# A planned first batch in which a load from DRAM waits, in the plan, for the landing of the store in front of it

## The chip, the cores and the metric

The kernel runs on one core of one Trainium2 chip. The metric is the device time of one execution in microseconds; three runs of the kernel before took 928.23, 928.39 and 931.25 us, median 928.39 us.

## The reference

A sparse attention of the Longformer kind feeds a two-layer feed-forward network, all in float32. There are 8 batches, 8 heads, 512 local and 32 global positions, and 64 elements in a head.

```python
s_g = scale * q_g @ k_all.T;  out_g = softmax(s_g) @ v_all      # 32 global rows see everything
mask = abs(pos[:, None] - pos[None, :]) <= 32                   # local rows: a band and the globals
s_l = concat([scale * q_l @ k_g.T, where(mask, scale * q_l @ k_l.T, -1e9)])
out_l = softmax(s_l) @ concat([v_g, v_l])
x = concat([out_g, out_l])                                      # 4608 tokens x 512
h = x @ w_in                                                    # 512 x 2048
g = maximum(h, 0) + alpha * minimum(h, 0)
out = g @ w_out                                                 # 2048 x 512
```

## The kernel before, in words

**Tiling.** The tokens form nine groups, one for the local tokens of each batch (512 tokens) and one for all global tokens. A group runs through 16 feed-forward blocks f of 128 hidden units. Step f1 makes the hidden block (h_ps) from the tokens, step f2 adds its part to the four output banks (o). f2 has two parts: fa uses the upper half gh of the activation (8 matmuls), fb the lower half gl (4 matmuls). Every float32 factor is split into an upper and a lower part, so that three products stand for one. Attention works on pairs P of heads, four to a batch and 32 in all. A batch's pairs must be through before its group's f1 steps begin.

**Weights.** The weights come as raw float64 words (`wraw`, 32 loads Lw of 512 KB) and are decoded on the chip in the first group's time: cv and ab on ScalarE (ACT), d1, d2, d3 on VectorE (DVE), ia on GpSimd (POOL), ca on ACT, su on DVE. Decoded second-layer weights are stored to DRAM (`wo`, and `wa` beside it), sums of first-layer weights too (`wf`), and read again in later groups.

**One pair in the first batch's time.** S makes the scores (s_ps). Pairs 0 to 3 are transposed on TensorE (T, Tg). Pairs 4 to 7 belong to batch 1 and go another way: red masks the scores into the tile `p` on DVE, ex exponentiates on ACT, nm normalises on POOL, and tq transposes 32x32 blocks in place on DVE. Then sq stores `p` to DRAM in four DMAs (tile `scratch`), and hq loads it back in the transposed layout (tile `pt`). The global part goes the same way: tr, sr (four DMAs from `sg_sb`) and hr. V multiplies `pt` with the values into o_ps, and G makes the next pair's global scores. The red step of pair P+1 overwrites `p` and so waits for sq of pair P. On the chip hq waits for the landing of sq's stores, and hr for that of sr's.

**What sets the order.** Nearly all DMAs of this stage, loads, stores and fetches, are issued by SyncE (SP) in program order. The order of the first batch's steps on each engine is written by a list scheduler, the class `Plan` (L59): `early` (L153) declares each step with engine, cost, needed steps, buffers taken and freed, and sometimes a due time. `due_times` (L70) works a due time back to every step and subtracts a bias by the step's name. `run` (L95) walks a model of the five engines: at each turn it takes the engine whose next step can start first, and on it, among the steps that could start within `near` of that time, the one with the earliest due time. Its start time is the end of each needed step plus a lag (L112). For two entries of SP that lag is -100: they count as ready at once. A DMA is taken to start 1.6 us after issue or behind the one before it, to last its `cost`, and to be seen 0.8 us later (L130, L131). The order that comes out is pinned; on the chip each engine follows it and waits where a step isn't ready. `issue` (L893) turns a name into instructions, `scatter` (L618) and `fetch_pt` (L629) are sq/sr and hq/hr. From block 16 on (L1114) the order is written in other functions, `slow_unit` and `fast_unit`, and left to the framework's own scheduler where not pinned. The numbers of the plan stand in LIST (L38): `first`, `pace`, `pair0` and `pair` set due times, `bias` shifts them.

Of the kernel before, what the change touches and what calls it, by code (L numbers as in the profile page):

```python
# [35 lines left out]
GOFF = 1024  # L36
GROWS = {1: (0, 0), 4: (0, 1), 7: (0, 2), 10: (1, 0), 13: (1, 1), 15: (1, 2)}
LIST = dict(  # L38
    first=37.579, pace=5.504, pair0=70.66, pair=20.171, slack=2, vsub=1, ahead=4, inflight=4, near=0.1, vgl=1, half=True,
    bias=dict(tq=-6, V=12, ex=-3, ca=-3, hr=6, gz=0, xB=12, hq=-1, Lw=-7, sr=12, ab=3, gsc=0, Lq=-6, be=5, rzr=1, yh=3, gexp=-12, cv=-1, ia=1, xA=3, red=-3),  # L40
)
FAST = range(2 * NF, NB * NF)
CATCH = (16, 23, 30)
# [15 lines left out]
class Plan:  # L59
# [3 lines left out]
        self.slots = {k: [0.0] * n for k, n in slots.items()}  # L63
        self.ops, self.slack, self.near, self.bias = {}, slack, near, bias

    def op(self, name, engine, cost, needs=(), lock=False, take=(), free=(), kind=None, due=None, n=1):
        assert name not in self.ops, name
        self.ops[name] = dict(engine=engine, cost=cost, needs=[x for x in needs if x], lock=lock, take=take, free=free, kind=kind, due=due, n=n)

    def due_times(self):  # L70
        users = {n: [] for n in self.ops}
# [23 lines left out]
    def run(self):  # L95
        ops, users = self.ops, self.due_times()
        end, order = {}, []
        free = dict(PE=5.4, ACT=2.5, DVE=5.0, POOL=4.0, SP=1.2)
        lock, dma, kind = 0.0, 3.3, None
        left = {n: len(o["needs"]) for n, o in ops.items()}  # L100
        ready = {n for n, k in left.items() if k == 0}
        while ready:
            can = []
            for n in sorted(ready):
                o = ops[n]
                e = o["engine"]
                if any(len(self.slots[p]) < k for p, k in o["take"]):
                    continue
                t = free[e]
                for x in o["needs"]:  # L110
                    y = ops[x]["engine"]
                    lag = (0.12 if e != "SP" else -100.0) if y == e else 0.3 if y == "PE" else 0.12  # L112
                    t = max(t, end[x] + lag)
                for p, k in o["take"]:
                    t = max(t, sorted(self.slots[p])[k - 1])
                if o["lock"]:
                    t = max(t, lock)
                can.append((t, o["at"], n))
            assert can, sorted(ready)
            t, _, n = min(can)  # L120
            e = ops[n]["engine"]
            t, _, n = min((c for c in can if ops[c[2]]["engine"] == e and c[0] <= t + self.near), key=lambda c: (c[1], c[0]))
            o = ops[n]
            cost = o["cost"]
            if e == "PE":
                cost = cost * (1.25 if t < 45 else 1.0) + (0.3 if kind != o["kind"] else 0.0)
                kind = o["kind"]
            if e == "SP":
                free[e] = t + 0.48 * o["n"]
                dma = max(dma, t + 1.6) + cost  # L130
                stop = dma + 0.8  # L131
            else:
                free[e] = stop = t + cost
                if o["lock"]:
                    lock = stop
            for p, k in o["take"]:
                for _ in range(k):
                    self.slots[p].remove(min(self.slots[p]))
            for p, k in o["free"]:
                self.slots[p] += [stop] * k  # L140
            end[n] = stop
            order.append(n)
            ready.discard(n)
            for u in users[n]:
                left[u] -= 1
                if left[u] == 0:
                    ready.add(u)
        assert len(order) == len(ops)
        self.end, self.order = end, order
        return order  # L150


def early(first, pace, pair0, pair, slack, vsub, ahead, inflight, near, vgl=0, half=False, bias={}):  # L153

    plan = Plan({"st": NST - 2, "w": NWB}, slack, near, bias)
    op = plan.op
    for P in range(9):
        pre = P < NRAW
        op(f"Lq{P}", "SP", 1.72, [f"G{P-2}", f"S{P-2}"] if P > 1 else [])
        if pre and P % 2:  # L160
            op(f"Lv{P}", "SP", 2.62, [f"S{P-1}"], take=(("w", 2),))
        else:
            op(f"Lv{P}", "SP", 2.62, [f"V{P-1 if P > NRAW else P-2}"] if P else [])
        due = pair0 + pair * (P - 5) if P > 4 else None
# [32 lines left out]
        last = first + pace * 15.5 if P == 8 else None  # L197
        if not pre:
            op(f"tq{P}", "DVE", 1.23, [f"nm{P}.0", f"nm{P}.1"], due=last)
            op(f"sq{P}", "SP", 1.31, [f"tq{P}"], n=4, due=last)  # L200
        if P == 8:
            break
        pb = [f"V{P-1}"] if P else []
        if pre:
            op(f"T{P}", "PE", 1.1, [f"nm{P}.0", f"nm{P}.1"] + ([f"pt0{P-1}", f"pt1{P-1}"] if P else []), kind="t", free=(("w", 1),) if P % 2 else ())
            op(f"pt0{P}", "ACT", 0.49, [f"T{P}"] + pb)
            op(f"pt1{P}", "DVE", 0.60, [f"T{P}"] + pb)
            op(f"Tg{P}", "PE", 0.45, [f"gsc{P}", f"T{P}", f"ptg{P-1}" if P else None], kind="t")
            op(f"ptg{P}", "ACT", 0.40, [f"Tg{P}"] + pb)
            lb = [f"pt0{P}", f"pt1{P}", f"ptg{P}"] + ([f"ex{P+1}.0", f"ex{P+1}.1"] if P < 3 else ["xlA1", "xlB1", "xg1"])  # L210
        else:
            op(f"tr{P}", "DVE", 0.5, [f"gsc{P}", "clear"])
            op(f"hq{P}", "SP", 1.31, [f"sq{P}"] + pb)
            op(f"sr{P}", "SP", 0.5, [f"tr{P}"], n=4)
            op(f"hr{P}", "SP", 0.5, [f"sr{P}", f"hq{P}"])
            lb = [f"hq{P}", f"hr{P}", f"mem{P+1}", f"Lq{P+1}"]
        op(f"V{P}", "PE", 2.0, [f"Lv{P}"] + lb, kind="v", free=(("w", 2),) if pre and P % 2 else ())
        if not pre:
# [7 lines left out]
        if not pre:  # L226
            c = P - NPAIR
# [8 lines left out]
    for k in range(2 * NF):  # L236
        f, j = divmod(k, 2)
# [12 lines left out]
    for t in range(NF):  # L250
        x = [f"xl{a}{P}" for P in range(NPAIR) for a in "AB"]
# [37 lines left out]
def longformer_ffn(ctx: ExitStack, tc: tile.TileContext, qk, v, w, alpha, out):  # L289
    nc = tc.nc  # L290
    pin, pin_sync = [True], [True]
    vec, act, pool = (Engine(tc, e, pin) for e in (nc.vector, nc.scalar, nc.gpsimd))
# [28 lines left out]
    sync = Engine(tc, nc.sync, pin_sync)  # L321
# [267 lines left out]
    def new_pt(P):  # L589
        if P not in pts:  # L590
            pts[P] = work.tile([128, 1408], F32, tag="pt", name="pt", bufs=1)
        return pts[P]
# [17 lines left out]
    scratch = {}  # L610

    def transpose_dve(P, x):
        t, n = (ps[P], 1024) if x == 0 else (sg_sb, 384)
        for e in range(0, n, 512):
            seg = t[:, e : min(n, e + 512)]
            vec.transpose(seg, seg)

    def scatter(P, x):  # L618
        t, n = (ps[P], 1024) if x == 0 else (sg_sb, 384)
        scratch[P, x] = dram.tile([4, 32, 4, n // 4], F32, tag=f"scratch{x}", name="scratch", bufs=2)  # L620
        for c in range(4):
            src = t[32 * c : 32 * c + 32, :].rearrange("k (j n) -> k j n", j=4)
            sync.dma_start(scratch[P, x][:, :, c, :].rearrange("j k n -> k j n"), src)

    def transpose_q(P, x):
        transpose_dve(P, x)
        scatter(P, x)

    def fetch_pt(P, x):  # L629
        sc = scratch.pop((P, x)).rearrange("j k c n -> (j k) (c n)")  # L630
        o, n = ((0, 1024), (GOFF, 384))[x]
        sync.dma_start(new_pt(P)[:, o : o + n], sc)

    def pv_all(P, first, last):
        vv, t = vs.pop(P), pts.pop(P)
# [247 lines left out]
    def begin():  # L883
# [3 lines left out]
        def parts(name):  # L887
            for k in ("tq", "sq", "hq", "tr", "sr", "hr", "Lq", "Lv", "Lw", "red", "mn", "ex", "rza", "rzr", "nm", "mem", "gm", "gexp", "gz", "gsc", "pt0", "pt1", "ptg", "Tg", "xlA", "xlB", "xA", "xB", "xg", "yh", "yl", "cv", "ab", "d1", "d2", "d3", "ia", "ca", "su", "wf", "wo", "f1", "fa", "fb", "gh", "gl", "S", "T", "V", "G", "p", "n", "mk", "al", "be"):
                if name.startswith(k) and name[len(k) :].replace(".", "").isdigit():
                    return k, name[len(k) :]  # L890
            return name, ""

        def issue(name):  # L893
            k, rest = parts(name)
            if k in ("red", "mn", "ex", "rza", "rzr", "nm"):
                P, h = map(int, rest.split("."))
# [7 lines left out]
            n = int(rest)  # L904
# [6 lines left out]
            if k in ("mk", "al", "be"):  # L911
                return
            if k in ("tq", "tr", "sq", "sr", "hq", "hr"):
                {"t": transpose_dve, "s": scatter, "h": fetch_pt}[k[0]](n, "qr".index(k[1]))
                return
            if k in ("cv", "ab", "d1", "d2", "d3", "ia", "ca", "su"):
                key = divmod(n, 2)
# [42 lines left out]
            elif k in ("xlA", "xlB"):  # L960
                a, src = (slice(0, 384), outs[n][0][:, 0:384]) if k == "xlA" else (slice(384, 512), outs[n][1][:, 0:128])
# [28 lines left out]
            else:  # L990
                raise KeyError(name)

        plan = early(**LIST)
        for name in plan.run():
            issue(name)
# [118 lines left out]
    for t in range(NF, NT + LAG):  # L1114
        G, f = divmod(t, NF)
# [75 lines left out]
```

## Time and profile before

| what | value |
|---|---|
| median of three runs | 928.39 us |
| the profiled execution's own time | 927.88 us |
| its span, first to last instruction | 926.1 us |
| TensorE busy | 885.9 us (96%) |
| VectorE busy | 608.7 us (66%) |
| ScalarE busy | 388.6 us (42%) |
| GpSimd busy | 312.7 us (34%) |
| mean granted TensorE clock | 0.972 |
| moved by DMA | 211.19 MB, mean 228 GB/s |

How to read it: PE is TensorE (PEld its weight loads), DVE is VectorE, ACT is ScalarE, POOL is GpSimd and SPq the DMA-issuing queue of SyncE. In a row of a timeline stand the start, the duration, engine, line, operation, what it writes and reads, how many were merged, and in brackets the idle time before it with what ended it. A row of waits names who waited for whom, the total, how often and the longest. Nearly all engine instructions have L280 and all matmuls L309, two helpers, so rows are told apart by their tiles. The work of the plan ends at about 180 us of the span.

### The profile page before, as it was taken

To read this page: it belongs to the slowest core of one execution; us is meant where nothing else is said; L and a number is where in the kernel's file an instruction comes from. 1 tells how busy PE (TensorE), PEld (TensorE's weight loads), DVE (VectorE), ACT (ScalarE), POOL (GpSimd) and SP (SyncE) were. 2 spreads that over 40 slices of the span, in tenths; PEclk is the share of its full clock that TensorE was granted. 3 is DMA by queue.
4 is the path that set the end of the run, shared out by engine and by line. 5 is a ranking of instruction groups with operands and counts; after the bars stand their busy time and mean duration, and the time that the engine had idled before them with its cause. 6 is when DMAs were issued, how large, how long until landed. Compare 5 with 4: busy or idle time off the path is not lost.

```text
span 926.1 us, 22539 instructions
## 1 busy us (share of the span) xinstructions
PE 885.9 (96%) x8668; PEld 764.9 (83%) x8668; DVE 608.7 (66%) x1676; ACT 388.6 (42%) x1166; POOL 312.7 (34%) x275
## 2 busy tenths in 40 slices
PE   7798968999999999999999999999999999999998
PEld 5676646787888888888888888888888899899898
DVE  5887757877577666866677667766686656544532
ACT  6877655553444433443345333443344322211211
POOL 3444433255444333433223323322343322222221
PEclk7889889799999999999999999999999999999999
DMA  8968977999665866586667667586657552645630
GB/s 306 348 178 322 341 252 271 337 362 358 232 208 177 294 210 197 189 277 217 211 228 253 230 224 225 187 262 217 201 181 269 185 192 91 205 160 180 205 116 24
DMA packets 86811, 211.19 MB, mean 228 GB/s; under 512 B 23985, under 2 KB 44465, under 8 KB 82865
## 3 DMA queue, kind: packets, MB, share of 16 engines
q1 hardware_dynamic: 86704, 209.76, 67.0%
q8 instruction: 68, 1.11, 0.5%
q14 instruction: 39, 0.31, 0.1%
HBM read 165.95 MB, written 43.78 MB: 226 GB/s over the span
## 4 chain that ended last, share of the span: by engine, by line
PE 67%; DMA 13%; DVE 9%; ACT 6%; SPq 2%; issue 2%; POOL 0%; DVEq 0%; ACTq 0%
PE o L309 30%; PE h_ps L309 28%; PE o_ps L309 4%; ACT p L280 3%; DMA scratch<-sg_sb 3%; PE s_ps L309 3%; DMA wraw<-in_w_dram 2%; PE g_ps L309 2%; DVE g L280 2%; DMA scratch<-p 2%; SPq L280 2%; DVE xl L280 2%; DMA pt<-scratch 1%; DMA alpha_sb<-in_alpha_dram 1%; DVE x_raw L280 1%
## 5 line engine op out<-in xcount | busy, mean ns | idle before, releaser
L280 POOL TENSOR_TENSOR gl<-g,gh 128x512 fp32r<-128x512 f32 (+1 forms) x128 | 159.1, 1243 | 375.8 <-ACT gh L280 306.0
L309 PE MATMUL h_ps<-xh,wt 128*128 128x256 f32 (+1 forms) x1120 | 241.0, 309 | 4.1 <-DVE wt L280 3.7
L309 PE MATMUL o<-gh,wo 128*128 128x512 f32 (+1 forms) x1024 | 244.3, 381 | 0.0
L280 ACT CAST gh<-g 128x512 fp32r<-128x512 f32 (+1 forms) x144 | 85.8, 596 | 306.5 <-DVE g L280 304.2
L309 PEld LDWEIGHTS o<-gh,wo 128*128 128x128 f32 x1024 | 176.8, 188 | 31.9 <-issue 0.4
L309 PEld LDWEIGHTS h_ps<-xh,wt 128*128 128x128 f32 x1120 | 182.4, 189 | 24.4 <-issue 6.1
L309 PE MATMUL h_ps<-xl,wt 128*128 128x256 f32 (+1 forms) x560 | 171.6, 306 | 0.8 <-DVE xl L280 0.8
L309 PE MATMUL o<-gl,wo 128*128 128x512 f32 (+1 forms) x512 | 131.1, 378 | 0.0
L280 DVE TENSOR_SCALAR g<-h_ps,alpha_sb 128x512 f32<-128x512 f32 (+1 forms) x128 | 91.5, 715 | 41.1 <-PE h_ps L309 35.4
L309 PEld LDWEIGHTS h_ps<-xl,wt 128*128 128x128 f32 x560 | 105.8, 189 | 6.6 <-DVE xl L280 1.0
L309 PE MATMUL h_ps<-xh,s 128*128 128x256 f32 x576 | 105.4, 279 | 2.9 <-DVE h_ps L280 2.0
L309 PEld LDWEIGHTS o<-gl,wo 128*128 128x128 f32 x512 | 92.8, 188 | 18.4
L280 POOL TENSOR_TENSOR p<-p,rz 128x512 f32<-128x512 f32 x64 | 69.2, 1101 | 101.1 <-DVE rz L280 95.2
L309 PEld LDWEIGHTS h_ps<-xh,s 128*128 128x128 f32 x576 | 90.7, 188 | 8.1 <-issue 4.0
L280 DVE TENSOR_TENSOR h_ps<-u,h_ps 128x256 f32<-128x256 f32 x144 | 61.1, 424 | 49.1 <-PE h_ps L309 47.5
L280 ACT ACTIVATE p<-p,mn 128x128 f32<-128x128 f32 x224 | 86.9, 396 | 4.8 <-DVE mn L280 4.8
L280 DVE SCALAR_TENSOR_TENSOR g<-h_ps,g 128x512 f32<-128x512 f32 (+1 forms) x128 | 84.1, 657 | 4.2
L309 PE MATMUL h_ps<-xl,s 128*128 128x256 f32 x288 | 80.6, 280 | 0.9 <-DVE xl L280 0.7
L280 DVE TENSOR_TENSOR u<-u,h_ps 128x256 f32<-128x256 f32 x96 | 40.3, 420 | 62.1 <-PE h_ps L309 38.7
L280 POOL TENSOR_TENSOR wt<-wt,wr 128x512 int32<-128x512 int32 x32 | 45.8, 1433 | 93.4 <-DVE wt L280 73.4
L309 PE MATMUL o_ps<-pt,v 128*64 128x32 f32 (+1 forms) x1600 | 59.8, 234 | 15.2 <-DMA pt<-scratch 13.2
L309 PEld LDWEIGHTS o_ps<-pt,v 128*64 128x64 f32 x1600 | 55.2, 149 | 22.4 <-DMA pt<-scratch 10.7
(88 smaller groups left out, 1046.1 us busy)
## 6 DMA issues: line engine op xcount, KB each, us to landing
wo<-wo SPq DMA_DIRECT2D x128, 512.0 KB, 4.4
v<-in_v_dram SPq DMA_DIRECT2D x30, 1024.0 KB, 5.8
qk<-in_qk_dram SPq DMA_DIRECT2D x32, 672.0 KB, 7.0
wraw<-in_w_dram SPq DMA_DIRECT2D x32, 512.0 KB, 7.4
scratch<-p SPq DMA_DIRECT2D x112, 128.0 KB, 3.0
pt<-scratch SPq DMA_DIRECT2D x28, 512.0 KB, 5.5
wo<-wt SPq DMA_DIRECT2D x16, 512.0 KB, 8.5
out_dram<-ost SPq DMA_DIRECT2D x32, 256.0 KB, 3.3
```

What stands on the lines that cost most here:

```text
L280: ins = op(*a, **k)
L309: ins = nc.tensor.matmul(*a, **k)
```

## The change

The lag between two SP entries stays at -100 except for steps whose name begins with h, which are hq and hr: they now start 0.12 us after the modelled end of the steps that they need, sq and for hr also sr and hq. The same line makes the lag between two TensorE steps 0.3 instead of 0.12. TensorE costs after 45 us are multiplied by 1.05, a DMA starts 2.0 instead of 1.6 us after issue. A step can now be a DMA issued by ACT (`dma=`), for names in `aq`; LIST sets `aq=""`, so all of them stay on SP. The numbers in LIST are others.

```diff
 LIST = dict(
-    first=37.579, pace=5.504, pair0=70.66, pair=20.171, slack=2, vsub=1, ahead=4, inflight=4, near=0.1, vgl=1, half=True,
-    bias=dict(tq=-6, V=12, ex=-3, ca=-3, hr=6, gz=0, xB=12, hq=-1, Lw=-7, sr=12, ab=3, gsc=0, Lq=-6, be=5, rzr=1, yh=3, gexp=-12, cv=-1, ia=1, xA=3, red=-3),
+    first=38.653, pace=5.504, pair0=72.073, pair=19.767, slack=2, vsub=1, ahead=4, inflight=4, near=0.1, vgl=1, half=True, aq="",
+    bias=dict(tq=-6, V=10, ex=-3, ca=-3, hr=9, xB=12, Lw=2, ab=3, Lq=3, be=5, rzr=13, yh=-9, gexp=-12, xA=-9, red=-3, fb=9, Lv=-6, p=-3, nm=12, ptg=1, mk=12, yl=-1, n=3, xlB=12, gh=3, xg=12, al=-3, sq=-12, xlA=12, T=-3, mn=3, mem=9, pt=-1, Tg=1),
 )
...
-                    lag = (0.12 if e != "SP" else -100.0) if y == e else 0.3 if y == "PE" else 0.12
+                    lag = -100.0 if y == e == "SP" and n[0] != "h" else 0.3 if y == "PE" else 0.12
...
-                cost = cost * (1.25 if t < 45 else 1.0) + (0.3 if kind != o["kind"] else 0.0)
+                cost = cost * (1.25 if t < 45 else 1.05) + (0.3 if kind != o["kind"] else 0.0)
...
-                dma = max(dma, t + 1.6) + cost
+                dma = max(dma, t + 2.0) + cost
                 stop = dma + 0.8
+            elif o["dma"]:
+                free[e] = t + cost
+                dma = max(dma, t + 2.0) + o["dma"]
+                stop = free[e] + 2.2 + 2 * o["dma"]
...
+    def move(name, dma, needs, n=1, due=None):
+        if name.rstrip("0123456789") in aq:
+            op(name, "ACT", 0.45 * n, needs, dma=dma, due=due)
+        else:
+            op(name, "SP", dma, needs, n=n, due=due)
...
-            op(f"sq{P}", "SP", 1.31, [f"tq{P}"], n=4, due=last)
+            move(f"sq{P}", 1.31, [f"tq{P}"], 4, last)
...
-            op(f"hq{P}", "SP", 1.31, [f"sq{P}"] + pb)
-            op(f"sr{P}", "SP", 0.5, [f"tr{P}"], n=4)
-            op(f"hr{P}", "SP", 0.5, [f"sr{P}", f"hq{P}"])
+            move(f"hq{P}", 1.31, [f"sq{P}"] + pb)
+            move(f"sr{P}", 0.5, [f"tr{P}"], 4)
+            move(f"hr{P}", 0.5, [f"sr{P}", f"hq{P}"])
```

`scatter` and `fetch_pt` get the queue as an argument, with SyncE as its default.

More of the change, by code (lines that the diff above doesn't have):

```diff
@@ L64, in __init__, with op @@
         self.ops, self.slack, self.near, self.bias = {}, slack, near, bias
-    def op(self, name, engine, cost, needs=(), lock=False, take=(), free=(), kind=None, due=None, n=1):
+    def op(self, name, engine, cost, needs=(), lock=False, take=(), free=(), kind=None, due=None, n=1, dma=None):
         assert name not in self.ops, name
-        self.ops[name] = dict(engine=engine, cost=cost, needs=[x for x in needs if x], lock=lock, take=take, free=free, kind=kind, due=due, n=n)
+        self.ops[name] = dict(engine=engine, cost=cost, needs=[x for x in needs if x], lock=lock, take=take, free=free, kind=kind, due=due, n=n, dma=dma)
     def due_times(self):
@@ L150, in run, with early @@
         return order
-def early(first, pace, pair0, pair, slack, vsub, ahead, inflight, near, vgl=0, half=False, bias={}):
+def early(first, pace, pair0, pair, slack, vsub, ahead, inflight, near, vgl=0, half=False, aq="sq sr hq hr", bias={}):
     plan = Plan({"st": NST - 2, "w": NWB}, slack, near, bias)
     op = plan.op
+    def move(name, dma, needs, n=1, due=None):
[3 more added lines that the diff above has]
+            op(name, "SP", dma, needs, n=n, due=due)
     for P in range(9):
@@ L616, in transpose_dve, with scatter @@
             vec.transpose(seg, seg)
-    def scatter(P, x):
+    def scatter(P, x, queue=sync):
         t, n = (ps[P], 1024) if x == 0 else (sg_sb, 384)
@@ L622, in scatter @@
             src = t[32 * c : 32 * c + 32, :].rearrange("k (j n) -> k j n", j=4)
-            sync.dma_start(scratch[P, x][:, :, c, :].rearrange("j k n -> k j n"), src)
+            queue.dma_start(scratch[P, x][:, :, c, :].rearrange("j k n -> k j n"), src)
     def transpose_q(P, x):
@@ L627, in transpose_q, with fetch_pt @@
         scatter(P, x)
-    def fetch_pt(P, x):
+    def fetch_pt(P, x, queue=sync):
         sc = scratch.pop((P, x)).rearrange("j k c n -> (j k) (c n)")
         o, n = ((0, 1024), (GOFF, 384))[x]
-        sync.dma_start(new_pt(P)[:, o : o + n], sc)
+        queue.dma_start(new_pt(P)[:, o : o + n], sc)
     def pv_all(P, first, last):
@@ L913, in issue @@
             if k in ("tq", "tr", "sq", "sr", "hq", "hr"):
-                {"t": transpose_dve, "s": scatter, "h": fetch_pt}[k[0]](n, "qr".index(k[1]))
+                if k[0] == "t":
+                    transpose_dve(n, "qr".index(k[1]))
+                else:
+                    {"s": scatter, "h": fetch_pt}[k[0]](n, "qr".index(k[1]), act if plan.ops[name]["engine"] == "ACT" else sync)
                 return
```

## The prediction

> **What bounds the kernel now.** I read the page first, then busy time by stage, then who waited for whom in the planned stage, then the engines' rows around the longest waits.
>
> ```profile
> span 926.1 us, 22539 instructions
> ...
> PEclk7889889799999999999999999999999999999999
> ```
>
> The clock row has 40 slices of 23.15 us, each digit the granted TensorE clock in tenths. All slices under 9 are among the first eight. Stage by stage:
>
> ```profile
> 44.00:120.00 76.00, 68.33 (x613) 53.12 (x613) 61.78 (x173) 54.34 (x139) 31.37 (x23) 0.91 0.83 291
> 120.00:170.00 50.00, 36.78 (x301) 28.89 (x302) 31.16 (x97) 27.49 (x76) 14.91 (x11) 0.81 0.78 264
> 186.00:926.10 740.10, 730.54 (x7029) 644.08 (x7027) 469.66 (x1281) 263.52 (x811) 244.35 (x208) 1.00 0.64 211
> ```
>
> The columns are the stage, its length, busy time of PE, PEld, DVE, ACT and POOL, the granted clock, the DMA share and GB/s. From 186 us TensorE is busy 730.54 of 740.10 us at clock 1.00. The change does not touch what runs there, so a microsecond won before reaches the end, and one lost too. The planned stage has 7.67 + 13.22 = 20.9 us of idle TensorE between 44 and 170 us; that and the clock there are all that the order can win behind the start. Who ends that idle time (44 to 185 us):
>
> ```profile
> PE o_ps L309 <- DMA pt<-scratch: 13.0, 5, 4.8
> PE h_ps L309 <- DVE wt L280: 3.7, 2, 2.6
> PE s_ps L309 <- DVE xl L280: 2.8, 1, 2.8
> PE o_ps L309 <- DMA scratch<-sg_sb: 1.3, 1, 1.3
> ```
>
> The first and the last row are one thing: the values step V (o_ps) stands at the head of TensorE's queue and its transposed probabilities, fetched back from DRAM, have not landed. The longest of these waits, for pairs 6 and 7, from the rows of TensorE around 130 and 160 us:
>
> ```profile
> 128.53 0.31 PE L309 MATMUL o_ps<-pt,v 128*64 128x32 f32 x4 [3.03 <-DMA pt<-scratch]
> 133.63 2.56 PE L309 MATMUL o_ps<-pt,v 128*64 128x64 f32 x44 [4.79 <-DMA pt<-scratch]
> ```
>
> ```profile
> 158.95 0.31 PE L309 MATMUL o_ps<-pt,v 128*64 128x32 f32 x4 [1.30 <-DMA scratch<-sg_sb]
> 162.13 2.13 PE L309 MATMUL o_ps<-pt,v 128*64 128x64 f32 x36 [2.87 <-DMA pt<-scratch]
> ```
>
> V6 waits 3.03 us before its first matmuls and 4.79 before the rest, V7 1.30 and 2.87: 12.0 of the 14.3. (The first piece ends with the local part that hq fetches, the second with the global part that hr fetches.) Their cause is on the sync queue, which issues in order:
>
> ```profile
> 115.92 3.26 SPq L280 DMA_DIRECT2D scratch<-p  x4
> 123.92 0.34 SPq L280 DMA_DIRECT2D pt<-scratch  x1
> 124.31 0.43 SPq L280 DMA_DIRECT2D wraw<-in_w_dram  x1
> 124.84 1.96 SPq L280 DMA_DIRECT2D scratch<-sg_sb  x4
> 131.09 0.34 SPq L280 DMA_DIRECT2D pt<-scratch  x1
> ```
>
> ```profile
> 154.72 0.34 SPq L280 DMA_DIRECT2D pt<-scratch  x1
> 155.17 1.79 SPq L280 DMA_DIRECT2D scratch<-sg_sb  x4
> 159.44 0.34 SPq L280 DMA_DIRECT2D pt<-scratch  x1
> 159.83 0.43 SPq L280 DMA_DIRECT2D wraw<-in_w_dram  x1
> ```
>
> After the four stores of pair 6 (115.92 + 3.26 = 119.18) nothing is issued until 123.92, when hq6 goes: 4.7 us. After sr6 (126.80) nothing until hr6 at 131.09: 4.3 us. Over the stage:
>
> ```profile
> SPq L280 <- DMA scratch<-p: 14.2, 6, 4.6
> ...
> SPq L280 <- DMA scratch<-sg_sb: 9.5, 4, 4.0
> ```
>
> That is 23.7 us in which the one queue that carries all loads stands behind a fetch whose store has not landed. The old plan charges no such wait between two sync entries (its lag is -100).
>
> **The change part by part.** The kernel computes the same with the same instructions; the list of the first batch is another. The cost goes by these parts.
>
> *Fetch behind the store's landing.* hq and hr become ready in the plan only when the store is taken to have landed, so whatever else is ready on sync (wraw, wf, wo, the next Lq or Lv) goes in front, and TensorE's list meets V later and puts ready f1 and f2 groups before it. No wait is added on the chip; four hq and four hr move back on sync and past no other queue. Behind hq6 stand one wraw, sr6 and hr6; behind hr7 a wraw that ACT waits for (below). What could TensorE run in the waits?
>
> ```profile
> 121.32 0.68 DVE L280 TENSOR_TENSOR gl<-g,gh 128x512 fp32r<-128x512 f32 x1
> ```
>
> ```profile
> 152.82 0.69 DVE L280 TENSOR_TENSOR gl<-g,gh 128x512 fp32r<-128x512 f32 x1
> ```
>
> ```profile
> 122.47 0.60 ACT L280 CAST gh<-g 128x512 fp32r<-128x512 f32 x1
> ```
>
> ```profile
> 156.70 0.60 ACT L280 CAST gh<-g 128x512 fp32r<-128x512 f32 x1
> ```
>
> ```profile
> 87.15 1.99 PE L309 MATMUL o<-gh,wt 128*128 128x512 f32 x8
> 88.98 1.08 PE L309 MATMUL o<-gl,wt 128*128 128x512 f32 x4
> ```
>
> Behind V6 stand one f2 part of four and one of eight matmuls (fb8, fa9), behind V7 fb11 and fa12; their gl and gh are ready at 122.0 and 123.1, and at 153.5 and 157.3, ahead of or in the waits. At full clock such a pair takes 1.08 + 1.99 = 3.07 us, so each of the two has 3.07 us of work that fits into its waits (7.82 and 4.17). **Term one: -6.1 us**, bounds 0 (V stays where it is in the list) and -12.0 (more is put in).
>
> *Clock.* What follows the waits runs at half clock:
>
> ```profile
> 134.00:140.00 6.00, 6.00 (x69) 4.83 (x66) 0.27 (x2) 1.00 (x2) 3.20 (x3) 0.50 1.02 356
> 164.00:172.00 8.00, 7.63 (x48) 5.64 (x47) 5.36 (x17) 6.81 (x22) 3.27 (x3) 0.52 1.00 355
> ```
>
> At full clock the 6.00 busy us at 0.50 would be 3.0 shorter, the 7.63 at 0.52 3.7: 6.7 in all. Filled by 3.07 each, V6's waits would be 4.75 and V7's 1.10, spread over two pieces each. I take half, **-3.3**, because I can't tell from one trace which gap sets the clock back; bounds 0 and -6.7. The Trainium skill ("TensorE: Matmul & The Clock Gate", section "HAM oscillation — how this bites in real kernels") says that idle gaps above about 3.4 us throttle TensorE. By that rule both come back whole if the 4.79 us gap is shortened to 1.72, and the sum below would be 3.4 us lower; the row at 0.52 behind gaps of 1.30 and 2.87 us fits the rule only if the two are counted together.
>
> *Loads in front of the fetch.* This is the price of the first part. The chain of work that ended last has one fetch behind a weight store (at 65 us) and one alone (at 131 us):
>
> ```profile
> 65.33 5.72 DMA pt<-scratch
> ```
>
> ```profile
> 131.09 2.50 DMA pt<-scratch
> ```
>
> Both are hr fetches; the first was issued right behind its own hq and a weight store (wo), the second after 4.3 us in which sync issued nothing. So a transfer put ahead of a fetch can make it land 3.2 us later. Between none and one for each of V6 and V7 gives 0 to +6.4; I take one, **+3.2**.
>
> *Decode.* The h_ps waits on wt (3.7 us) stand where DVE waits for a store in front of the next mask step. The better plan can put decode in front of it. I take **-1.0**, bounds 0 and -3.7. The rest of the diff (PE cost times 1.05, 0.3 instead of 0.12 us between two PE steps, DMA start 2.0 instead of 1.6, new biases) only changes which of two nearly ready steps is first. What that does to the 0 to 44 us stretch no row shows; I take 0, bounds -2.8 and +2.8, the one wait of TensorE on xl above. The queue argument "aq" names no step, so all transfers stay on sync.
>
> What is late next: ACT.
>
> ```profile
> 164.06 0.67 ACT L280 ACTIVATE wr<-wraw 128x512 int32<-128x512 uint32 x1 [6.23 <-DMA wraw<-in_w_dram]
> ```
>
> ACT stands 6.23 us for the wraw that sync issues at 159.83, behind hr7; a cast of h_ps that later f1 steps need is queued behind it. V7's wait covers that today. If V7 no longer waits, this wraw must be issued ahead of hq7, or the 4.2 us of V7 come back as a wait for it. That the plan now holds hq7 back until landing lets the load go first.
>
> **Sum:** -6.1 - 3.3 + 3.2 - 1.0 = -7.2 us. The profiled execution took 927.88 us (1.8 around its span of 926.1) against a median of 928.39, 0.5 more. 927.88 - 7.2 = 920.7, plus 0.5 is **921.2 us**.
>
> **The rivals.**
> - *Slower: the fetches starve.* Transfers pushed in front of hq and hr make both of a pair land 3.2 us later, and hr, which the plan now also holds until hq has landed, is issued later than the chip needs. On three pairs (5 to 7) with one pushed transfer each that reaches V: 3 × 3.2 = 9.6, less 1.0 of decode and less 3.07 of filler in one wait: +5.5, **934 us**. It decides as soon as V keeps its place in TensorE's order while its fetch moves back. For it: windows of DMA share 1.00 and 1.02 above, in which any added transfer must queue. Against it: the DMA share of the whole stretch from 120 to 170 us is 0.78, so there are holes to fill. [...]
> - *No difference.* The list changes, but V still waits for the same chain, and the f2 groups put in front are missed behind it. Sync's blocked time moves to other entries. Terms cancel: **928 us**. The change not doing what it says falls here too: if the modelled landing comes earlier than the measured one, hq still blocks sync.
> - *Much faster.* The plan fills all waits on V6 and V7 (12.0), the clock stays up (6.7), decode is never late (3.7), and one pushed fetch costs 3.2: -19.2, **909 us**. For it: 23.7 us of blocked sync. Against it: DVE is busy 61.78 of 76.00 us before 120, so it can't run far ahead.
>
> **How the numbers follow.** About 0.3% (2.8 us) is what a measurement can tell from no change. Chances: forecast 0.42, much faster 0.18, no difference 0.15, starved fetches 0.25. Of the forecast's cases some 0.02 fall within 0.3%, of the starved ones 0.01: faster 0.58, same 0.18, slower 0.24. The range leaves out a tenth at each end: the upper end takes in most of the starved case with its own spread of one more pushed fetch less the start's gain, 933; the lower the much faster case but for its far half, 909. The forecast's own range is 914 to 925.
>
> **What would show it.** Right: sync's waits for scratch<-p and scratch<-sg_sb fall from 23.7 us to under 12; a wraw, wf or wo stands between a pair's stores and its hq; V6 and V7 wait under 6 us together; the clock stays above 0.8 from 130 to 172; TensorE is in its steady stretch about 7 us earlier. Starved: sync's waits fall, but pt<-scratch lands later and TensorE's wait for it grows beyond 14.3. Wrong altogether: the waits on V are the same and the start, before 48 us, has moved by several us.

## The result and the profile after

Four runs of the changed kernel took 915.54 to 919.29 us, median 916.45, against a median of 928.83 for four runs of the kernel before (928.23 to 931.25). The ratio is 0.987, 95% interval 0.983 to 0.990: faster by 12.4 us, where 7.2 were forecast. The profiled execution of the changed kernel is its slowest, 919.29 us, so the two profiled executions differ by 8.6 us only, and the reading below explains those. Matmuls now have L320 and the other engine instructions L291.

The page of the changed kernel, span and clock row:

```profile
span 917.4 us, 22516 instructions
...
PEclk7899999989999999999999999999999999999999
```

Before, six of the first eight slices were under 9. Now two are, and the ninth, which begins at 183 us; that one is V8's, below. Busy time by stage (stage, length, PE, PEld, DVE, ACT, POOL, granted clock, DMA share, GB/s):

```profile
44.00:120.00 76.00, 69.94 (x636) 55.28 (x637) 68.86 (x197) 58.55 (x148) 33.22 (x25) 0.96 0.93 317
120.00:170.00 50.00, 42.68 (x408) 33.34 (x408) 41.95 (x102) 32.06 (x79) 18.03 (x14) 0.97 0.90 319
170.00:200.00 30.00, 24.85 (x215) 20.23 (x214) 17.79 (x50) 13.70 (x40) 15.23 (x14) 0.89 1.00 376
```

Between 44 and 170 us TensorE idles 13.4 us instead of 20.9, and the clock is up from 0.91 and 0.81 to 0.96 and 0.97. Work at full clock is busy time times clock: from 120 to 170 us it was 36.78 × 0.81 = 29.8 us and is 42.68 × 0.97 = 41.4; from 44 to 120 it was 62.2 and is 67.1. That is 16.5 us more, some 7 by less idling and some 9 by the clock. TensorE's waits from 44 to 185 us (who, for what, total, times, longest):

```profile
PE h_ps L320 <- DVE wt L291: 6.3, 2, 4.2
PE g_ps L320 <- ACT x_raw L291: 4.3, 2, 3.4
...
PE o_ps L320 <- DMA pt<-scratch: 0.9, 1, 0.9
```

The waits of V4 to V7 (o_ps) fell from 14.3 us to 0.9. V6 has the 0.9, V7 waits for nothing. The sync queue in the same stretch:

```profile
SPq L291 <- DMA scratch<-sg_sb: 5.5, 4, 2.1
...
SPq L291 <- DMA scratch<-p: 3.1, 5, 1.0
```

ACT's wait for raw weights, before and after:

```profile
ACT wr L280 <- DMA wraw<-in_w_dram: 22.8, 11, 6.2
```

```profile
ACT wr L291 <- DMA wraw<-in_w_dram: 9.8, 5, 3.0
```

Sync stood 23.7 us behind stores that had not landed, now 8.6, and ACT's total wait for raw weights fell from 22.8 us to 9.8. What went into the freed time shows in sync's own rows at pair 7:

```profile
127.41 3.48 SPq L291 DMA_DIRECT2D scratch<-p  x4
130.98 0.40 SPq L291 DMA_DIRECT2D wf<-wt  x1
131.42 0.69 SPq L291 DMA_DIRECT2D wraw<-in_w_dram  x1
132.26 0.58 SPq L291 DMA_DIRECT2D v<-in_v_dram  x1
134.49 0.33 SPq L291 DMA_DIRECT2D pt<-scratch  x1
```

Between the four stores and their fetch now stand a sum store, a raw load and a load of values. The price, in the DMA issues from 44 to 180 us (KB each, median us from issue to landing), before and after:

```profile
pt<-scratch SPq DMA_DIRECT2D x4, 512.0 KB, 4.2
pt<-scratch SPq DMA_DIRECT2D x4, 192.0 KB, 2.6
```

```profile
pt<-scratch SPq DMA_DIRECT2D x5, 512.0 KB, 6.4
pt<-scratch SPq DMA_DIRECT2D x5, 192.0 KB, 3.4
```

The rows after count pair 8's two fetches as well, which went before 180 us. For pairs 4 to 7 alone (issues from 44 to 158 us) the medians after are 7.2 and 3.1 us: a local fetch takes 3.0 us longer from issue to landing, a global one 0.5, and V hardly notices.

So the plan's stage went better than forecast, and yet the spans differ by 8.7 us only. Two marks show where the rest stayed. The first is fb13, an f2 step (o<-gl) near the end of the plan; the second is V8, the values of the first pair behind it, which is not in the plan. Before:

```profile
180.46 1.08 PE L309 MATMUL o<-gl,wt 128*128 128x512 f32 x4
...
196.50 1.59 PE L309 MATMUL o_ps<-pt,v 128*64 128x32 f32 x48
```

After:

```profile
163.54 1.08 PE L320 MATMUL o<-gl,wt 128*128 128x512 f32 x4
...
185.05 2.56 PE L320 MATMUL o_ps<-pt,v 128*64 128x64 f32 x44 [5.15 <-DMA pt<-scratch]
```

fb13 comes 16.9 us earlier. At V8 TensorE stands 5.15 us for a fetch, which it did not do before, and the 4 us behind that wait run at half clock (0.50), worth 2 more: 16.9 - 5.15 - 2 = 9.8. From 230 us on TensorE has 677.92 us of busy time left, 686.72 before: 8.8 of lead, 1.0 less than that sum, and it stays at that to the end (8.7). The wait is for hr8, the last fetch of pair 8. The chain of waits has it last before V8, and sync's rows show what stands in front of it:

```profile
165.12 11.23 DMA wo<-wo
...
177.30 7.70 DMA pt<-scratch
```

```profile
172.35 0.34 SPq L291 DMA_DIRECT2D wsum<-wf  x1
173.06 0.34 SPq L291 DMA_DIRECT2D wo<-wo  x1
175.07 0.32 SPq L291 DMA_DIRECT2D wo<-wt  x1
176.37 0.32 SPq L291 DMA_DIRECT2D wo<-wo  x1
176.73 0.45 SPq L291 DMA_DIRECT2D wsum<-wf  x1
177.30 0.38 SPq L291 DMA_DIRECT2D pt<-scratch  x1
```

Five weight transfers go right ahead of it, the DMA share there is 1.00, and it takes 7.70 us to land, where the global fetches of pairs 4 to 7 take 3.1. The chain also names what held sync up ahead of it: a weight load (wo) that was issued at 165.12 us and took 11.23 to land; only then did the last two transfers and hr8 go. For sr8's stores sync shows no wait from 160 to 178 us. Why sync stood until that load had landed the profile doesn't show. Before, pair 8's fetches were issued at 182.00 us (hr8) and 184.36 (hq8) and V8 stood at 196.50, so both had landed well ahead of it.

### The profile page after: what moved, and what is told of

Its sections match the earlier page's. It is cut to its first block, busy times and chain, and to the rows that moved or that the text cites. A ratio compares the mean times of both kernels' runs of the same rounds, so it can differ in the third digit from the quotient of the medians.

```text
span 917.4 us, 22516 instructions
## 1 busy us (share of the span) xinstructions
PE 880.7 (96%) x8666; PEld 762.1 (83%) x8668; DVE 609.2 (66%) x1676; ACT 390.0 (43%) x1166; POOL 312.4 (34%) x275
## 4 chain that ended last, share of the span: by engine, by line
PE 69%; DVE 12%; DMA 9%; ACT 6%; issue 1%; SPq 1%; POOL 0%; DVEq 0%; ACTq 0%; POOLq 0%
PE o L320 31%; PE h_ps L320 28%; PE o_ps L320 4%; PE s_ps L320 3%; ACT p L291 3%; DVE g L291 3%; DMA wraw<-in_w_dram 2%; DVE xl L291 2%; PE g_ps L320 2%; DMA scratch<-sg_sb 2%; DMA wo<-wo 1%; DVE x_raw L291 1%; DVE wt L291 1%; SPq L291 1%; DMA v<-in_v_dram 1%
## 5 line engine op out<-in xcount | busy, mean ns | idle before, releaser
L291 POOL TENSOR_TENSOR gl<-g,gh 128x512 fp32r<-128x512 f32 (+1 forms) x128 | 158.9, 1242 | 380.5 <-ACT gh L291 311.4
L320 PE MATMUL h_ps<-xh,wt 128*128 128x256 f32 (+1 forms) x1120 | 241.6, 310 | 6.8 <-DVE wt L291 6.3
L320 PE MATMUL o<-gh,wo 128*128 128x512 f32 (+1 forms) x1024 | 245.0, 381 | 0.0
L291 ACT CAST gh<-g 128x512 fp32r<-128x512 f32 (+1 forms) x144 | 85.8, 596 | 316.2 <-DVE g L291 308.5
L320 PEld LDWEIGHTS h_ps<-xh,wt 128*128 128x128 f32 x1120 | 182.6, 189 | 26.7 <-DVE wt L291 7.2
L320 PEld LDWEIGHTS o<-gh,wo 128*128 128x128 f32 x1024 | 177.3, 188 | 32.2 <-issue 0.6
L320 PE MATMUL h_ps<-xl,wt 128*128 128x256 f32 (+1 forms) x560 | 171.5, 306 | 0.8 <-DVE xl L291 0.8
L320 PE MATMUL o<-gl,wo 128*128 128x512 f32 (+1 forms) x512 | 131.0, 378 | 0.0
L291 DVE TENSOR_SCALAR g<-h_ps,alpha_sb 128x512 f32<-128x512 f32 (+1 forms) x128 | 91.7, 716 | 43.4 <-PE h_ps L320 37.5
L320 PEld LDWEIGHTS h_ps<-xl,wt 128*128 128x128 f32 x560 | 106.0, 189 | 6.7 <-DVE xl L291 1.0
L320 PE MATMUL h_ps<-xh,s 128*128 128x256 f32 x576 | 105.6, 279 | 2.8 <-DVE h_ps L291 2.0
L320 PEld LDWEIGHTS o<-gl,wo 128*128 128x128 f32 x512 | 92.8, 188 | 18.4
L291 POOL TENSOR_TENSOR p<-p,rz 128x512 f32<-128x512 f32 x64 | 71.2, 1130 | 108.2 <-DVE rz L291 103.9
L320 PEld LDWEIGHTS h_ps<-xh,s 128*128 128x128 f32 x576 | 90.8, 188 | 8.1 <-issue 3.9
L291 DVE TENSOR_TENSOR h_ps<-u,h_ps 128x256 f32<-128x256 f32 x144 | 61.1, 424 | 49.4 <-PE h_ps L320 47.8
L291 DVE SCALAR_TENSOR_TENSOR g<-h_ps,g 128x512 f32<-128x512 f32 (+1 forms) x128 | 84.2, 658 | 4.3
L291 ACT ACTIVATE p<-p,mn 128x128 f32<-128x128 f32 x224 | 86.9, 396 | 0.5 <-DVE mn L291 0.3
L291 DVE TENSOR_TENSOR u<-u,h_ps 128x256 f32<-128x256 f32 x96 | 40.3, 420 | 63.2 <-PE h_ps L320 37.9
L320 PE MATMUL h_ps<-xl,s 128*128 128x256 f32 x288 | 80.6, 280 | 0.9 <-DVE xl L291 0.8
L291 POOL TENSOR_TENSOR wt<-wt,wr 128x512 int32<-128x512 int32 x32 | 43.6, 1363 | 67.6 <-DVE wt L291 47.4
L320 PEld LDWEIGHTS o_ps<-pt,v 128*64 128x64 f32 x1600 | 53.9, 147 | 14.0 <-DMA pt<-scratch 6.3
L320 PE MATMUL o_ps<-pt,v 128*64 128x32 f32 (+1 forms) x1600 | 58.4, 232 | 6.9 <-DMA pt<-scratch 6.0
```

Source lines behind the costliest of these rows:

```text
L291: ins = op(*a, **k)
L320: ins = nc.tensor.matmul(*a, **k)
```

## The experiments

The theory after the result: the fetch behind its store's landing keeps sync and TensorE going, and what it wins is decided behind the plan, at V8. Rivals: the searched numbers in LIST make the gain, not the lag; the filler in front of V makes it, wherever the fetch stands; or the later fetch alone does. Ratios are against runs of the kernel before on the same chip, with 95% intervals. "Median (n)" gives the runs.

### The lag alone, the numbers alone, the model alone

Kernel before, with the new lag for hq and hr and nothing else (the lag between two TensorE steps stays at 0.12):

```diff
-                    lag = (0.12 if e != "SP" else -100.0) if y == e else 0.3 if y == "PE" else 0.12
+                    lag = (0.12 if e != "SP" or n[0] == "h" else -100.0) if y == e else 0.3 if y == "PE" else 0.12
```

> The kernel before with one edit: in the plan hq and hr wait for the modelled landing of their stores; costs, biases and due times stay the old ones. If the wait in the plan is the cause of the gain: sync's waits for scratch<-p and scratch<-sg_sb between 44 and 185 us fall from 23.7 us to under 12, TensorE's waits for pt<-scratch fall from 14.3 us to under 5, and the time comes to 915 to 921 us. If the newly searched numbers are the cause: 926 us or more.

929.53 us (10), ratio 0.998 (0.995 to 1.001): no difference, where 915 to 921 us were expected of the lag. But the stage did what the theory says: sync's waits for the two scratch stores are 7.2 us, TensorE's for pt<-scratch before 185 us are 0.2. Its last planned group, G8 (the global scores of pair 8) and V8:

```profile
164.18 1.08 PE L309 MATMUL o<-gl,wt 128*128 128x512 f32 x4
...
165.29 0.67 PE L309 MATMUL g_ps<-qk 128*64 128x288 f32 x6
...
191.99 2.56 PE L309 MATMUL o_ps<-pt,v 128*64 128x64 f32 x44 [10.54 <-DMA pt<-scratch]
```

fb13 is 16.3 us earlier than before, nearly as early as in the changed kernel, and V8 then stands 10.54 us. G8 runs at 165.29, behind fb13; in the changed kernel it runs at 158.21, in front of it, and in the kernel before too, at 167.98. From G8 come the scores that sr8 stores and hr8 fetches: sr8 is issued at 175.33 us here and at 165.78 in the changed kernel, hr8 at 186.91 and 177.30.

Kernel before, with the changed kernel's LIST and nothing else:

```diff
-    first=37.579, pace=5.504, pair0=70.66, pair=20.171, slack=2, vsub=1, ahead=4, inflight=4, near=0.1, vgl=1, half=True,
+    first=38.653, pace=5.504, pair0=72.073, pair=19.767, slack=2, vsub=1, ahead=4, inflight=4, near=0.1, vgl=1, half=True,
...
```

The line of biases, left out here, is the changed kernel's too.

> The kernel before with the new numbers of LIST (due times and biases), the old model: hq and hr count as ready at once. If the wait in the plan is the cause, this gives less than half of the gain: 923 us or more. If the search is the cause: 915 to 919 us.

932.49 us (10), ratio 1.002 (1.000 to 1.004). V6 and V7 wait 8.87 and 4.47 us, the clock from 120 to 170 us is 0.76. Yet the stage from 44 to 120 us goes better (clock 0.97), and fb13 stands at 173.93, 6.5 us earlier than before; V8 then waits 6.80 us. By the median the numbers without the lag bring nothing.

Changed kernel, with the LIST of before (and `aq=""`):

```diff
-    first=38.653, pace=5.504, pair0=72.073, pair=19.767, slack=2, vsub=1, ahead=4, inflight=4, near=0.1, vgl=1, half=True, aq="",
+    first=37.579, pace=5.504, pair0=70.66, pair=20.171, slack=2, vsub=1, ahead=4, inflight=4, near=0.1, vgl=1, half=True, aq="",
...
```

Again the line of biases goes with it.

> The kernel after with the old numbers of LIST: the new model (hq and hr wait for landing, TensorE costs times 1.05, DMA start 2.0 us, 0.3 us between two TensorE steps). If the model is the cause: 914 to 920 us. If the search is the cause: 925 us or more.

936.09 us (5), ratio 1.007 (1.004 to 1.009): slower. fb13 at 165.34, 15.1 us earlier than before; V8 waits 12.64 us. By the medians lag and numbers are each worth nothing alone, and together 12 us; in all three profiles V8 takes back most of what fb13 had won.

### G8's place

If lag alone loses at V8 because G8 stands late, moving G8 alone must bring the gain, and moving it back in the changed kernel must take it away. The lag-only kernel, with G8 ahead of f115 and fb13, and the steps behind it on other engines earlier too:

```diff
+        order = plan.run()
+        for name, behind in (("xg7", "xB7"), ("G8", "xg7"), ("gm8", "yl3"), ("gexp8", "f115"), ("gz8", "d229"), ("gsc8", "d329")):
+            order.remove(name)
+            order.insert(order.index(behind) + 1, name)
...
```

> The kernel with the lag alone, and pair 8's global scores G8 (with gm8, gexp8, gz8, gsc8 behind it) moved ahead of the last two feed-forward groups of the plan, as the searched numbers place them. Theory now: the lag alone already brings TensorE through the plan 15 us earlier, and V8, outside the plan, gives it back, because its global fetch hangs on G8, which the lag alone puts last. Then V8's wait falls from 10.5 us to 5 to 7 us and the time from 929.5 to 921 to 925 us. Rival: V8's fetch is late because the DMA engines are full from 160 us on; then V8's wait stays at 9 us or more and the time at 927 to 930 us.

919.55 us (6; 914.26 to 924.96), ratio 0.988 (0.984 to 0.993), with the old numbers in LIST. G8 at 160.01, sr8 at 166.19, hr8 at 174.37, and V8 doesn't wait, where 5 to 7 us were expected:

```profile
180.98 1.59 PE L309 MATMUL o_ps<-pt,v 128*64 128x32 f32 x48
```

The changed kernel, with G8 and its softmax steps behind fb13:

```diff
+        order = plan.run()
+        for name, behind in (("G8", "fb13"), ("Lq10", "G8"), ("gm8", "p15"), ("gexp8", "gh15"), ("gz8", "gl15"), ("gsc8", "gz8")):
+            order.remove(name)
+            order.insert(order.index(behind) + 1, name)
...
```

> The kernel after with G8 and its softmax steps moved to the end of the plan. If G8's place is what the searched numbers bought at the end of the plan: V8's wait grows from 5.15 us to 9 us or more and the time to 921 to 926 us. If the DMA engines set it: the wait stays at 5 to 6 us, time 916 to 919 us.

932.34 us (10), ratio 1.002 (0.999 to 1.004): the whole gain is gone. fb13 is even earlier, at 160.09:

```profile
161.09 0.70 PE L320 MATMUL g_ps<-qk 128*64 128x288 f32 x6
...
189.13 2.56 PE L320 MATMUL o_ps<-pt,v 128*64 128x64 f32 x44 [10.14 <-DMA pt<-scratch]
```

sr8 goes at 171.74, 6.0 us later than in the changed kernel. The time is above the 921 to 926 us that were expected: besides V8's wait TensorE idles 4.1 us from 200 to 230 us, where the changed kernel doesn't idle. Of all that the new numbers move, the place of G8 and its softmax steps is what decides; the two edits move these together, so they don't tell G8 from the steps behind it.

### The fetch back, the filler alone, the late fetch alone

The changed kernel, with hq and hr of pairs 4 to 7 put right behind their stores, as early as the buffers allow:

```diff
+        order = plan.run()
+        for P in range(NRAW, 8):
+            for name, behind in ((f"hq{P}", (f"sq{P}", f"V{P-1}")), (f"hr{P}", (f"sr{P}", f"hq{P}"))):
+                order.remove(name)
+                order.insert(max(order.index(x) for x in behind) + 1, name)
...
```

> The kernel after with each hq and hr issued on sync right behind its stores (hr also behind its hq), all other orders as they are. If the place of the fetch on sync is what counts: sync's waits for the two scratch stores return to 20 us or more, loads come late, and the time rises to 924 us or more. If it is TensorE's order, in which V comes later, that counts: the time stays at 916 to 919 us.

930.35 us (10), ratio 1.002 (1.000 to 1.005): the gain is gone. Sync's waits are back, above those of before:

```profile
SPq L291 <- DMA scratch<-sg_sb: 14.7, 5, 5.3
SPq L291 <- DMA scratch<-p: 13.1, 6, 6.5
```

V waits only 0.3 us, since V still stands late. Instead the decode starves: ACT waits 24.2 us for raw weights and TensorE 12.1 for decoded ones.

The kernel before, with the f2 parts that stood behind V put in front of it, and sync's order as it was:

```diff
+        order = plan.run()
+        for P, fill in ((4, ("fb1", "fa2")), (5, ("fa5",)), (6, ("fb8", "fa9")), (7, ("fb11", "fa12"))):
+            for name in fill:
+                order.remove(name)
+                order.insert(order.index(f"V{P}"), name)
...
```

> The kernel before with the ready second-layer groups put in front of V on TensorE (fb1 and fa2 before V4, fa5 before V5, fb8 and fa9 before V6, fb11 and fa12 before V7), sync as it was. Term one of the prediction says that this alone saves 6.1 us in V's waits and some of the clock: 919 to 924 us. If the loads held up on sync are the bound, the filler only moves the wait to the next step that needs decoded weights: 926 to 930 us.

928.72 us (10), ratio 0.999 (0.997 to 1.001): nothing. TensorE's waits from 44 to 185 us:

```profile
PE h_ps L309 <- DVE wt L280: 8.0, 6, 4.1
PE o_ps L309 <- DMA pt<-scratch: 4.1, 1, 4.1
PE g_ps L309 <- ACT x_raw L280: 3.9, 1, 3.9
```

The waits on V fell from 14.3 us to 4.1, and the waits on the decode took their place (h_ps 3.7 to 8.0, g_ps 0.4 to 3.9). As long as sync is blocked (16.9 + 8.3 us here), the raw weights come late, and TensorE meets that somewhere.

The kernel before, with each hq and hr moved behind up to three further entries of sync's list, and V where it was:

```diff
+        for P in range(NRAW, 8):
+            for name in (f"hr{P}", f"hq{P}"):
+                at = order.index(name)
+                later = [x for x in order[at + 1 : order.index(f"V{P}")] if plan.ops[x]["engine"] == "SP" and x != f"hr{P}"]
+                if later:
+                    order.remove(name)
+                    order.insert(order.index(later[min(2, len(later) - 1)]) + 1, name)
...
```

> The kernel before with hq and hr moved back on sync behind up to three further entries, TensorE's order as it was. If the place of the fetch on sync counts by itself: sync's waits for the stores fall under 14 us and the time to 918 to 923 us. If V's place in TensorE's order counts: V waits for a fetch that lands later, 14.3 us of waits become 16 or more, and the time is 926 to 935 us (the starved fetches of the prediction).

933.68 us (10), ratio 1.004 (1.002 to 1.006): slower. Sync waits only 1.8 us for these stores, but 37.2 us for TensorE's steps on g_ps, 13.3 before. ACT's wait for raw weights falls to 3.7 us, and V still waits 13.2 us for its fetches, and 5.0 more for other things (decoded weights, issue). So V keeps its place, its fetch moves back, and the kernel gets slower, as the rival of the starved fetches has it. But not on its path: the waits of V4 to V7 for their fetches did not grow (13.2 us, 14.3 before; 16 or more were expected), and V8 comes at 197.49 us, only 1.0 later than before, while the span of this profile (935.2 us) is 9.1 longer. Most of that arises behind the plan: pair 9's values wait 3.72 us for their global fetch, until 227.50, and TensorE runs at clock 0.79 from 220 to 230 us and at 0.86 in the next 10.

### V8

The wait of V8 that is left in the changed kernel was attacked in three ways. First, a later place for V8. CATCH lists the blocks behind the plan in which two steps of the attention are taken instead of one; its first entry goes from block 16 to 19, in the changed kernel and in the kernel before:

```diff
-CATCH = (16, 23, 30)
+CATCH = (19, 23, 30)
```

> The kernel after with one number changed behind the plan: the doubled attention step moves from block 16 to block 19 (CATCH), so that V8 comes one block later on TensorE. In the profile after, V8 waits 5.15 us for its fetch at 179.9 us and the next 5 to 6 us run at half clock. If that is where part of the gain is given back: the wait falls under 2 us and the time to 908 to 913 us. If the DMA engines, busy 0.98 of the time there, are the bound, the wait moves to a later step and the time stays at 915 to 918 us.

> The kernel before with the same number changed. V8 does not wait there, so both theories expect no change: 927 to 930 us.

In the changed kernel the wait falls from 5.15 to 3.34 us and the time is 917.13 us (4), ratio 0.984 (0.982 to 0.987), within the interval of the changed kernel as it is: 1.8 us less of waiting, and no gain that these runs could show. In the kernel before with the same edit, where V8 waits for nothing, the time is 931.45 us (10), ratio 1.000 (0.999 to 1.002).

Second, the weight sums of the next group loaded four blocks later, so that hr8 has less in front of it:

```diff
-        if NF <= t < 2 * NF and t % 2 == 0:
-            load_sums((t - NF) // 2)
+        if NF + 4 <= t < 2 * NF and t % 2 == 0:
+            load_sums((t - NF - 4) // 2)
...
-        if NF + 2 <= t < 2 * NF and t % 2 == 0:
-            weight_sums((t - NF - 2) // 2)
+        if NF + 6 <= t < 2 * NF and t % 2 == 0:
+            weight_sums((t - NF - 6) // 2)
...
```

> The kernel after with the eight loads of weight sums (512 KB each, needed from block 32 on) and their arithmetic four blocks later, so that none of them stands in front of V8's fetch. If full DMA engines and SP's order in front of hr8 make V8 wait: the wait falls under 3 us and the time to 910 to 914 us. If V8's chain is bound by its own steps (G8, softmax, transpose, store, load): wait and time stay, 915 to 918 us.

927.70 us (10), ratio 0.998 (0.995 to 1.000): the opposite of what was expected. The sync rows in front of hr8:

```profile
172.67 2.07 SPq L291 DMA_DIRECT2D wo<-wo  x3
174.78 0.43 SPq L291 DMA_DIRECT2D wsum<-wf  x1
175.26 0.95 SPq L291 DMA_DIRECT2D wo<-wo  x2
176.56 0.34 SPq L291 DMA_DIRECT2D wsum<-wf  x1
177.06 0.32 SPq L291 DMA_DIRECT2D pt<-scratch  x1
```

There is no hole: behind the plan the framework's scheduler orders what isn't pinned, and it put five weight loads and two sums ahead of hr8 there. hr8 is issued at the same time, lands 9.7 us after that (7.70 in the changed kernel), and V8 waits 8.73.

Third, hr8 in the plan itself: hq8 behind the last sum store, the transposes of the scores behind su29, hr8 at the plan's end, and the order of the first blocks behind it pinned on sync:

```diff
+            if name == "wf15":
+                fetch_pt(8, 0)
+            if name == "su29":
+                transpose_q(8, 1)
+        fetch_pt(8, 1)
...
+            if s == 3 and P == 8:
+                return
...
+        pin_sync[0] = t < NF + 3
```

> The kernel after with pair 8's remaining transfers (hq8, sr8, hr8) issued in the plan, and sync held to program order up to block 18, so that none of the loads for batch 1 (wo, wsum) stands in front of hr8. If the transfers in front of hr8 make V8 wait: V8's wait falls from 5.15 us to under 2 us, the clock behind it stays up, and the time comes to 908 to 913 us. If sync then stands behind hr8's store and the loads held back come late for batch 1: a new wait of 4 us or more for wo or for pair 9 appears before 230 us and the time is 916 to 922 us.

913.51 us (6; 909.92 to 916.06), ratio 0.983 (0.980 to 0.986), the fastest kernel of the study. Sync and TensorE:

```profile
164.13 1.80 SPq L291 DMA_DIRECT2D scratch<-sg_sb  x4
165.97 0.43 SPq L291 DMA_DIRECT2D wo<-wt  x1
166.44 0.45 SPq L291 DMA_DIRECT2D wa<-wt  x1
169.32 0.33 SPq L291 DMA_DIRECT2D pt<-scratch  x1
```

```profile
170.00:200.00 30.00, 30.00 (x249) 24.39 (x248) 16.57 (x56) 14.53 (x53) 11.76 (x12) 1.00 0.98 355
```

Two weight stores and no load stand between sr8 and hr8, which goes 8 us earlier than in the changed kernel. V8 doesn't wait:

```profile
178.48 1.59 PE L320 MATMUL o_ps<-pt,v 128*64 128x32 f32 x48
```

From 170 to 200 us TensorE is busy throughout at clock 1.00, where the changed kernel has 24.85 us at 0.89; from 200 to 230 us it idles 2.25 us, 1.4 of them at pair 9's fetch. The edit makes three steps at once, and its median is 2.9 us under the changed kernel's, with intervals that overlap a little, so the runs alone don't prove the gain over the changed kernel.

## Why the prediction was right, and where it wasn't

The time, 916.45 us, lies in the range of 909 to 933 and is 4.75 us under the 921.2. That the stated sum comes this near is in part luck (below).

**The mechanism** holds: each sign that was named came. Sync's waits for its stores are 8.6 us (under 12 was named), a sum store, a raw load and a load of values stand before hq7, V6 and V7 wait 0.9 us (under 6), the clock from 130 to 172 us is 0.96 (above 0.8), and TensorE has 8.8 us of lead from 230 us on (about 7). That it takes the late fetch and the late V together is shown by fb13 in the runs that do one of them, against 180.46 us before: 179.99 with the filler alone, 181.38 with the late fetch alone, 177.29 with the fetch put back; the lag, which does both, has it at 164.18. The medians (0.999, 1.004, 1.002) could not show it by themselves, since the lag alone has 0.998.

**Term one** (-6.1, bounds 0 and -12.0) was too small: V6 and V7 lost 11.1 of 12.0 us, all four pairs 13.4 of 14.3. The prediction counted as filler the f2 parts that stand behind V in the old list. That more work becomes ready with sync free fits ACT's shorter waits; no run shows it by itself. The stage's idle time fell by 7.5 only, because other waits of TensorE rose (decode, below).

**The clock** (-3.3, bounds 0 and -6.7) was too small as well, by more than its bound: some 9 us of the 16.5 that the stage gained. The prediction priced the two windows behind V6 and V7 only. The stage from 44 to 120 us gained too, 0.91 to 0.96.

**The pushed fetch** (+3.2) is there, +3.0 us for the local and +0.5 for the global fetches of pairs 4 to 7 in the medians, but V stands late enough that only 0.9 us of it is seen. **Decode** (-1.0) had the wrong sign: the waits on wt rose from 3.7 to 6.3 us, and those of g_ps on x_raw from 0.4 to 4.3. **ACT's wait for wraw** went as argued, by loads ahead of the fetch. **The start** moved little: the plan's first fb part (o<-gl) begins at 60.3 us instead of 61.7.

**The failed step** is "The change does not touch what runs there, so a microsecond won before reaches the end". Of 16.9 us won at fb13, 8.7 reach the end of the profiled execution. Old code behind the plan bounds it: hr8 is issued by its own chain (G8, sr8, then what stands ahead on sync), and what TensorE wins it then waits for at V8. With the lag alone 16.3 us are won, V8 waits 10.54, and the median is that of before. That the sum of -7.2 is near the profiles' -8.6 is luck, two errors that cancel: the gain in the plan twice as large, and half of it given back.

The second failed step: the other numbers "only change which of two nearly ready steps is first". That is so, and it was priced at nothing; but one of these steps is G8, and its place, with that of its softmax steps, is worth the whole change, as the two runs that move them show in both directions (0.988 with them early and nothing else of the numbers, 1.002 with them late).

**The starved fetches**, the slower rival, decide "as soon as V keeps its place in TensorE's order while its fetch moves back". The kernel with just that edit is slower, by 0.4% where 0.6% was named. The size is near by chance: the named path, longer waits of the pairs in the plan, did not come; in its profile most of the loss is at pair 9, behind the plan.

For the lag alone the books close too: 16.3 us less 10.54 at V8, less 3.3 by the clock from 170 to 200 us (19.46 us busy at 0.83) and 1.8 of idle TensorE from 200 to 230 would leave 0.7 won, and its profile has 689.12 us of busy time left at 230 us, 2.4 more than before. These 3 us are found in the next stretch: TensorE waits 2.35 and 1.23 us for the steps of the following pair's scores (s_ps, at 230.55 and 232.30 us), and from 230 to 240 us it is busy 8.22 us at clock 0.66, which is 2.8 us more than at full clock.

Open stays why the changed kernel's profiled execution lies 2.8 us above its median; one profile can't tell. Not tried was hr8 in the plan without the transposes or the pinned order.

## What to carry to other kernels

Here a load that reads back a store blocked its whole queue until the store had landed (23.7 us of sync); a plan that put ready transfers in that time, and ready matmuls in front of the consumer, won twice, but each alone won nothing (0.999 and 1.004). A gain in one stage is worth what the first fixed due point behind it lets through: follow each chain (here G8, sr8, hr8, V8) to the first consumer outside the stage before counting it as won. Moving loads out of the way of a fetch helped here only where the order was pinned; where it wasn't, the scheduler had put others in their place.

## What the runs showed of the hardware

How short a gap lowers the clock was not expected. The kernel before has, at 90 us, a gap of 2.62 us with no other in the 12 us before it, and this is the clock behind it:

```profile
92.92 0.66 PE L309 MATMUL h_ps<-xh,wt 128*128 128x512 f32 x1 [2.62 <-DVE wt L280]
```

```profile
92.90:96.00 3.10, 3.08 (x8) 2.41 (x9) 2.10 (x11) 0.78 (x2) 1.57 (x1) 0.53 0.94 317
```

From 80 us to its end the clock was 1.00, the 3.1 behind it at 0.53, and the next 4 at 0.93. The Trainium skill ("TensorE: Matmul & The Clock Gate", section "HAM oscillation — how this bites in real kernels") puts the limit at idle gaps above about 3.4 us; this gap is shorter and the clock behind it is down, so the measurement decides. Length alone doesn't settle it: a gap of 2.09 us in the changed kernel, ending at 122.53, left the clock at 1.00 in the 4.5 us behind it. The prediction's clock term counted the two long gaps only; that shorter ones such as this were part of what it missed fits, but no run took one of them alone.

A 192 KB fetch took 2.50 us to land alone (kernel before, 131.09 us), 5.72 behind its pair's fetch and a weight store (65.33), and 7.70 behind five weight transfers in a stretch with a DMA share of 1.00 (changed kernel, 177.30).
